# Attention scores from the third pair on in three passes of rounded parts, with the parts made on POOL

## The chip, the cores and the metric

The kernel runs on one core of a Trainium2 chip. The metric is the device time of one execution, in microseconds (us). The time before the change is the median of three runs, 790.76 us (790.69 to 790.87).

## What is computed

A causal attention block is followed by two mixing blocks; all tensors are float32. Sizes: batch 2, 12 heads, sequence 448, head width 64, model width 768, hidden width 3072, rank 32.

```
scores = (q @ k.T) / sqrt(64); causal mask; softmax over keys
x      = softmax(scores) @ v, heads side by side       # 2 x 448 x 768
h      = x.T @ U @ V                                    # mixes tokens
u      = x + h.T
y      = u + relu(u @ w_ch1) @ w_ch2
out    = y + relu(layernorm(y) * g @ w_ch1b) @ w_ch2b
```

## The kernel before

TensorE (PE in the profile) does nearly all of the work. The attention takes the first 99 us, the two feed-forward layers the rest.

**The attention** works on pairs of heads: 2 batches by 6 pairs are 12 pairs, numbered n = 0 to 11. A tile `qk` holds q and k of a pair, transposed: partitions 0 to 63 are the first head, 64 to 127 the second. `a_load(n)` (L307) fetches it with two DMAs on SP's queue; the pool has three buffers. `a_scores(n)` (L328) multiplies four blocks of 112 query rows with the keys up to the diagonal, for both heads: eight matmuls with 448, 336, 112 and 224 columns in turn, each 64 rows deep, so that the two heads use the two halves of the array's rows. Their operands are plain float32. A float32 matmul shows in the trace as two MATMUL records, so one pair has 16. At its end `a_scores(n)` starts `a_load(n + 3)`.

`a_max` (L349) on DVE (VectorE) then adds the mask and takes row maxima, eight instructions per pair at L357. `a_exp` (L366) on ACT (ScalarE) takes the exponentials. `a_transpose` (L379) turns the weights over on PE (20 transposes, L392), copies them out on DVE (L396) and ACT (L401), and has POOL (GpSimd) add a small number to the row sums (`rd`, L382). `a_values` (L403) multiplies with v (L412). `a_tokens` (L419), `a_mix1` (L447) and `a_mix2` (L466) lay the result out by tokens and begin the mixing with U and V; `a_mix1` has ACT and DVE write a small tile `ts` (L459, L462), which the last matmul of `a_mix2` (L476) reads.

**The order of the work** is written by hand. The loop over n (L533) handles pair n's transposes and values, the tokens of pair n - 1, the mixing of pair n - 2 and the scores and maxima of pair n + 2 in the same round. The prologue computes the scores of pairs 0 and 1. One round from n = 3 on takes the same 8.12 us each time.

**Weights ahead of time.** The feed-forward weights arrive as 64-bit numbers in tiles `raw`, fetched on SP's queue by `load` (L79). ACT takes their magnitude (L126), and DVE narrows them to float32 in four steps over 768 columns (`narrow`, L130): two tensor_scalar instructions on one tensor (L138, L141), then two scalar_tensor_tensor instructions on two tensors (L143, L145). In the attention's rounds `weights(9999, 2, ...)` (L406) puts at most two such steps at the end of a round of DVE.

**The other matmuls** (L490, L681, L815) already work with high and low parts: a tensor is rounded to the type F32R (high part), the rest is stored as a second F32R tensor (low part), and three passes high x high, high x low and low x high are summed. An F32R matmul shows as one MATMUL record. `low_part` (L199) makes the low part, in the attention on POOL, later on DVE.

The scores before, as they are issued:

```python
    for (h, i), (acc, o) in sorted(at.items(), key=lambda t: turns.index(t[0][1])):
        w = (i + 1) * Q
        r = slice(h * D, (h + 1) * D)
        nc.tensor.matmul(
            acc[:Q, o:o + w], t[r, 0, i * Q:(i + 1) * Q], t[r, 1, :w], start=True, stop=True,
        )
    a_load(n + 3)
```

Of the kernel before, what the change touches and what calls it, by code (L numbers as in the profile page):

```python
# [9 lines left out]
F32R = mybir.dt.float32r  # L10
# [3 lines left out]
ALU = mybir.AluOpType  # L14
PSUM = bass.MemoryType.PSUM

B, H, S, D = 2, 12, 448, 64
# [4 lines left out]
P = 128  # L22
Q = 112
# [20 lines left out]
def block_kernel(ctx: ExitStack, tc: tile.TileContext, qk, v, U, V4, w1a, w2a, w1b, w2b, g_ln, out):  # L44
    nc = tc.nc
    f32 = lambda ap: ap.bitcast(F32)
# [13 lines left out]
    attn = ExitStack()  # L60
    attn_c = attn.enter_context(tc.tile_pool(name="attn_c", bufs=1))

    def bank(name):
        return ps.tile([P, 512], F32, tag="bank", name=name)
# [44 lines left out]
    def magnitude():  # L109

        if len(started) > (not now[0]) or not (to_start and raws):
            return False
        m, n = to_start[0]
        if m and n % 2 == 0:
            if len(x_open) >= X_BUFS and x_open[-X_BUFS]:
                return False
            x_s[0] = x_w.tile([P, 2, DM], F32, tag="x", name=f"x{m}_{n}")
            x_open.append(2)
        to_start.pop(0)
        t, rows, cols = raws.pop(0)  # L120
        low, high = (t[:rows, :cols].bitcast(U32).rearrange("p (n t) -> p n t", t=2)[:, :, i] for i in range(2))
        x = x_s[0][:, n % 2] if m else uv[n][:rows, :cols]
        if m:
            x_of[m, n] = len(x_open) - 1
        act(cols)
        nc.scalar.activation(x, high.bitcast(F32), AF.Abs)  # L126
        started.append((x, x_s[0], low, high))
        return True
# [21 lines left out]
    def whole(steps):  # L150
        while True:
            try:
                next(steps)
            except StopIteration as e:
                return e.value
# [138 lines left out]
                return  # L294

    qk_p = attn.enter_context(tc.tile_pool(name="qk_p", bufs=2))
    s_p = attn.enter_context(tc.tile_pool(name="s_p", bufs=6))
    pt_p = attn.enter_context(tc.tile_pool(name="pt_p", bufs=6))
    x_p = attn.enter_context(tc.tile_pool(name="x_p", bufs=2))
    ot_p = attn.enter_context(tc.tile_pool(name="ot_p", bufs=2))  # L300
    sel_p = attn.enter_context(tc.tile_pool(name="sel_p", bufs=1))

    sc_t, qk_t, v_t, s_t, den_t, pt_t, x_t, o_t, rd_t, nm_t = ({} for _ in range(10))
    pairs = [(b, p) for b in range(B) for p in range(NP)]
    NPT = len(pairs)

    def a_load(n):  # L307

        if n >= NPT:
            return  # L310
        r = qk_t[n] = qk_p.tile([P, 2, S], F32, tag="qk", name=f"qk{n}", bufs=3)
        src = qk[n].rearrange("p (a h s) -> p a h s", a=2, h=2)
        for part in (slice(0, 2 * Q), slice(2 * Q, S)) if n == 0 else (slice(0, S),):
            for h in range(2):
                rows = slice(h * D, (h + 1) * D)
                (nc.scalar if h and n == 0 else nc.sync).dma_start(out=r[rows, :, part], in_=src[rows, :, h, part])
# [8 lines left out]

    JOBS = [[(h, 3, 0)] for h in range(2)] + [[(h, 2, 0), (h, 0, 336)] for h in range(2)] + [[(h, 1, 0)] for h in range(2)]

    def a_scores(n):  # L328
        if n >= NPT:
            return  # L330
        t = qk_t.pop(n)
        sc_t[n] = [bank("sc") for _ in JOBS]
        at = {(h, i): (acc, o) for acc, job in zip(sc_t[n], JOBS) for h, i, o in job}
        turns = (3, 2, 0, 1) if n else (1, 0, 2, 3)
        for (h, i), (acc, o) in sorted(at.items(), key=lambda t: turns.index(t[0][1])):
            w = (i + 1) * Q
            r = slice(h * D, (h + 1) * D)
            nc.tensor.matmul(  # L338
                acc[:Q, o:o + w], t[r, 0, i * Q:(i + 1) * Q], t[r, 1, :w], start=True, stop=True,
            )  # L340
        a_load(n + 3)


    TURNS = [(m, h, i, o) for m, job in enumerate(JOBS) for h, i, o in job]
# [1 line left out]
    def turns_of(n):  # L346
        return TURNS if n else sorted(TURNS, key=lambda t: (t[1], (1, 0, 2, 3).index(t[2])))

    def a_max(n, between=None):  # L349

        if n < NPT:
            nm = nm_t[n] = small.tile([Q, 2, NQ], F32, tag="nm", name=f"nm{n}")
            sb = s_t[n] = [s_p.tile([Q, OFF[NQ]], F32, tag="s", name=f"s{n}_{h}") for h in range(2)]
            accs = sc_t.pop(n)
            for k, (m, h, i, o) in enumerate(turns_of(n)):
                w = (i + 1) * Q
                nc.vector.tensor_tensor_reduce(  # L357
                    sb[h][:, OFF[i]:OFF[i + 1]], accs[m][:Q, o:o + w], mask[:, S - w:], -0.125, 3.0e38,
                    ALU.add, ALU.min, accum_out=nm[:, h, i:i + 1],
                )  # L360
                if k == 5 and between:
                    next(between)
        if between:
            whole(between)

    def a_exp(n):  # L366

        if n >= NPT:
            return
        den = den_t[n] = small.tile([Q, 2, NQ], F32, tag="den", name=f"den{n}")  # L370
        nm, sb = nm_t.pop(n), s_t[n]
        for _, h, i, _ in turns_of(n):
            s = sb[h][:, OFF[i]:OFF[i + 1]]
            nc.scalar.activation(  # L374
                s, s, AF.Exp, bias=nm[:, h, i:i + 1], scale=-1.0, accum_out=den[:, h, i:i + 1]
            )
            yield
# [69 lines left out]
    def a_mix1(n):  # L447

        b, p = pairs[n]
        x = x_t[b, p // 2]  # L450
        c = (p % 2) * P
        acc = bank("t4")
        for i in range(NQ):
            nc.tensor.matmul(acc[:, :P], u_r[:, i * P:(i + 1) * P], x[:, i, c:c + P], start=i == 0, stop=i == NQ - 1)  # L454
        acc_t = acc
        t = ts[b][:, p * P:(p + 1) * P]

        def parts():
            nc.scalar.copy(t, acc_t[:, :P])  # L459
            yield  # L460
            r = slice(2 * R, P)
            nc.vector.tensor_tensor(t[r], acc_t[r, :P], f32(t[r]), ALU.subtract)  # L462

        return parts()
# [35 lines left out]
    with tc.manual_schedule():  # L500
# [15 lines left out]
        t = wraw.tile([P, DM], I64, tag="raw64", name="raw64")  # L516
# [11 lines left out]
        for _ in a_exp(0):  # L528
            pass
        a_scores(1)  # L530
        a_max(1)
        early, low = {}, None
        for n in range(NPT):  # L533
            exps = a_exp(n + 1)
            if n == 0:
                magnitude()
                magnitude()
            a_transpose(n, exps, low)
            if n:
                a_tokens(n - 1)  # L540
            mix = a_mix1(n - 2) if n > 1 else None
            a_scores(n + 2)
            if n == 0:
                u_n = whole(narrow())[0].rearrange("p (i r) -> p i r", i=NQ)
                nc.gpsimd.tensor_copy(
                    u_r.rearrange("p (i g r) -> p i g r", i=NQ, g=4), u_n.unsqueeze(2).to_broadcast([Q, NQ, 4, R])
                )
                v_n = whole(narrow())[0]
            if n == NPT - 1:
                early[0] = bank("h")  # L550
                mm1(early[0], 0, 0, S, range(KC // 2))
            if n >= NPT - 2:
                next(mix)
            for _ in range(3):
                next(exps, None)
            high_parts(nc.gpsimd)
            a_max(n + 2, mix)
            for _ in exps:
                pass
            if n == NPT - 1:  # L560
                mm1(early[0], 0, 0, S, range(KC // 2, KC))
            a_values(n)
            if n == 0:

                v_r = bank("vr")
                for g in range(4):
                    nc.tensor.matmul(  # L567
                        v_r[:, g * Q:(g + 1) * Q], sel[:, g].rearrange("p a r -> p (a r)"), v_n,
                        start=g == 0, stop=g == 3, skip_group_check=True,
                    )  # L570
                nc.scalar.copy(vs, v_r[:, :S])
                for g in (1, 3):
                    r = slice(g * R, (g + 1) * R)
                    nc.vector.tensor_tensor(vs[r], v_r[r, :S], f32(vs[r]), ALU.subtract)
                nc.gpsimd.memset(f32(vz).bitcast(U32), 0)
                nc.gpsimd.tensor_copy(vz[:, 0, :64], f32(vs[:, 384:448]))
                nc.gpsimd.tensor_copy(vz[:, 1, 64:], f32(vs[:, 0:64]))
            a_load_v(n + 3)
            if n > 1:
                low = a_mix2(n - 2)  # L580
# [284 lines left out]
        for layer in range(2):  # L865
            building, s_t = None, []
            for g in range(NG):
# [35 lines left out]
                if (layer, g) in FAST:  # L903
# [7 lines left out]
                    turns = [(0, 1), (0, 2), (0, 6), (0, 5), (0, 7), (1, 1), (0, 4), (1, 2), (0, 3), (1, 6), (1, 5), (1, 7)]  # L911
# [14 lines left out]
                else:  # L926
# [7 lines left out]
                    for slot, (j, half) in enumerate(jobs):  # L934
                        n = ns[j]
# [3 lines left out]
                        if half == 0 and n in early:  # L939
                            acc = early[n]  # L940
                        else:
                            acc = bank("h")
# [109 lines left out]
```

## Time and profile before

| | |
|---|---|
| median of three runs | 790.76 us |
| the profiled execution's own time | 789.65 us |
| its span, first to last instruction | 787.9 us |
| PE busy | 782.8 us, 99% of the span |
| DVE busy | 638.1 us, 81% |
| ACT busy | 406.6 us, 52% |
| POOL busy | 109.7 us, 14% |
| granted TensorE clock, mean over the span | 1.000 |

The profiled execution took 1.11 us less than the median, and 1.75 us of its time lie outside the span. Busy time of an engine counts instructions that overlap once. A PE record's start is when it was let go, and its end is modelled, so an array that waits a short while can still read as busy.

### The profile page before, as it was taken

Reading aid. Unit: us, or ns where it says so; the run is one execution under the profiler, and the core shown is the slowest. Engines: PE = TensorE matmul, PEld = TensorE weight load, DVE = VectorE, ACT = ScalarE, POOL = GpSimd, SP = SyncE. Lnnn points to the kernel's source line nnn. Section 1 sums busy time; section 2 is a strip of 40 time slices with the busy share of each in tenths; the row PEclk is TensorE's granted clock in tenths of the full one; section 3 lists DMA queues with packets and bytes.
Section 4 is the critical chain, followed back from the end, with each engine's and each line's share of the span. In section 5 each row is a group of like instructions: output and inputs, shape, how many; then the busy total and the mean of one; then the engine's idle time right before and its main releaser. Section 6 shows DMA issues by size and latency. Waiting matters only on the chain.

```text
span 787.9 us, 12054 instructions
## 1 busy us (share of the span) xinstructions
PE 782.8 (99%) x4510; PEld 728.7 (92%) x4510; DVE 638.1 (81%) x1114; ACT 406.6 (52%) x817; POOL 109.7 (14%) x136
## 2 busy tenths in 40 slices
PE   9999999999999999999999999999999999999998
PEld 7777789998999999999999999989999999999997
DVE  6888869979988969789698789988989698697532
ACT  6988936353555464364463544635554544643510
POOL 1010130110210300301202501201202202103000
PEclk9999999999999999999999999999999999999999
DMA  8564344892683862944927425946946828628234
GB/s 203 171 166 120 94 144 162 182 239 80 152 230 105 222 172 83 272 110 124 289 78 268 164 81 153 236 118 179 225 132 165 216 92 221 172 96 182 39 124 157
DMA packets 39258, 126.45 MB, mean 160 GB/s; under 512 B 4752, under 2 KB 14816, under 8 KB 39200
## 3 DMA queue, kind: packets, MB, share of 16 engines
q1 hardware_dynamic: 25936, 97.24, 37.0%
q0 software_dynamic: 12656, 27.99, 21.1%
q8 instruction: 35, 0.57, 0.3%
q10 hardware_dynamic: 608, 0.46, 0.2%
q14 instruction: 23, 0.19, 0.1%
HBM read 89.88 MB, written 35.78 MB: 159 GB/s over the span
## 4 chain that ended last, share of the span: by engine, by line
PE 99%; DVE 0%; ACT 0%; issue 0%; POOL 0%; POOLq 0%
PE y L681 44%; PE pA L815 15%; PE h L490 15%; PE pB L815 7%; PE pC L815 4%; PE sc L338 3%; PE pv L412 3%; PE tr L392 3%; PE t L454 1%; PE uT L472 1%; PE xt L424 1%; PE zT L747 1%; PE warm L525 0%; PE uT L476 0%; PE y L710 0%; PE vr L567 0%
## 5 line engine op out<-in xcount | busy, mean ns | idle before, releaser
L681 PE MATMUL y<-w,h 128*128 128x384 f32 x2016 | 354.9, 334 | 0.0
L681 PEld LDWEIGHTS y<-w,h 128*128 128x128 f32 x2016 | 349.7, 188 | 1.3 <-DVE u L758 0.3
L490 PE MATMUL h<-u,w 128*128 128x384 f32 (+2 forms) x576 | 118.3, 364 | 0.0
L201 DVE TENSOR_TENSOR w<-x,w 128x768 fp32r<-128x768 f32 x93 | 87.1, 951 | 35.2 <-ACT w L190 35.2
L490 PEld LDWEIGHTS h<-u,w 128*128 128x128 f32 x576 | 104.9, 188 | 10.7
L126 ACT ACTIVATE x<-raw 128x768 f32<-128x768 f32 x96 | 86.7, 911 | 48.9 <-DMA raw<-in_w2b 25.0
L698 POOL DMA_DIRECT2D ysum<-part x54 | 47.2, 875 | 419.2 <-ACT part L697 417.4
L143 DVE SCALAR_TENSOR_TENSOR x<-raw,x 128x768 uint32<-128x768 uint32 x96 | 91.9, 957 | 2.6
L145 DVE SCALAR_TENSOR_TENSOR x<-raw,x 128x768 uint32<-128x768 uint32 x96 | 91.7, 955 | 2.1
L697 ACT COPY part<-y 128x384 f32<-128x384 f32 x108 | 46.5, 484 | 86.6 <-PE y L681 55.3
L190 ACT CAST w<-x 128x768 fp32r<-128x768 f32 x96 | 76.4, 838 | 9.6 <-PE h L490 4.5
L138 DVE TENSOR_SCALAR x<-x 128x768 f32<-128x768 f32 x96 | 54.7, 569 | 12.8 <-ACT x L126 12.6
L141 DVE TENSOR_SCALAR x<-x 128x768 uint32<-128x768 uint32 x96 | 53.6, 558 | 1.9
L374 ACT ACTIVATE s<-s,nm 112x336 f32<-112x336 f32 (+2 forms) x96 | 50.7, 536 | 0.0
L357 DVE CUSTOM_DVE_ANT_0 s<-sc,mask 112x336 f32<-112x336 f32 (+2 forms) x96 | 36.5, 445 | 12.8 <-PE sc L338 12.8
L823 ACT COPY u<-pA 128x448 f32<-128x448 f32 x32 | 17.1, 534 | 49.1 <-PE pA L815 45.9
L692 POOL DMA_DIRECT2D ysum<-part x32 | 29.7, 1071 | 58.5 <-ACT part L691 58.5
L765 ACT ACTIVATE h<-h 128x384 fp32r<-128x384 f32 (+2 forms) x32 | 17.5, 546 | 37.9 <-PE h L490 37.9
L767 DVE SCALAR_TENSOR_TENSOR h<-u,h 128x448 fp32r<-128x448 f32 x32 | 20.0, 626 | 17.7 <-ACT h L765 17.7
L815 PE MATMUL pC<-u,w 128*128 128x448 f32 x144 | 32.1, 367 | 0.0
L815 PE MATMUL pB<-u,w 128*128 128x448 f32 x144 | 32.0, 366 | 0.0
L815 PE MATMUL pA<-u,wt 128*128 128x448 f32 x144 | 32.0, 366 | 0.0
(105 smaller groups left out, 970.3 us busy)
## 6 DMA issues: line engine op xcount, KB each, us to landing
ysum<-part POOLq DMA_DIRECT2D x54, 384.0 KB, 7.0
raw<-in_w1a SPq DMA_DIRECT2D x24, 768.0 KB, 6.5
raw<-in_w2a SPq DMA_DIRECT2D x24, 768.0 KB, 4.9
raw<-in_w1b SPq DMA_DIRECT2D x24, 768.0 KB, 5.8
raw<-in_w2b SPq DMA_DIRECT2D x24, 768.0 KB, 4.8
ysum<-part POOLq DMA_DIRECT2D x32, 192.0 KB, 6.6
y<-ysum SPq DMA_DIRECT2D x14, 384.0 KB, 4.0
qk<-in_qk SPq DMA_DIRECT2D x22, 224.0 KB, 3.9
```

What stands on the lines that cost most here:

```text
L126: nc.scalar.activation(x, high.bitcast(F32), AF.Abs)
L138: nc.vector.tensor_scalar(x, x, LEAST, GREATEST, ALU.max, ALU.min)
L141: nc.vector.tensor_scalar(bits, bits, 5, 2, ALU.logical_shift_left, ALU.logical_shift_right)
L143: nc.vector.scalar_tensor_tensor(bits, low, 29, bits, ALU.logical_shift_right, ALU.bitwise_or)
L145: nc.vector.scalar_tensor_tensor(bits, high, 0xC0000000, bits, ALU.bitwise_and, ALU.bitwise_or)
L190: nc.scalar.copy(w[:, 0], x)
L201: engine.tensor_tensor(w[:, 1], x, f32(w[:, 0]), ALU.subtract)
L374: nc.scalar.activation(s, s, AF.Exp, bias=nm[:, h, i:i + 1], scale=-1.0, accum_out=den[:, h, i:i + 1])
L490: nc.tensor.matmul(acc[:, :width], w[:, a, k, c0:c0 + P], u[:, c, kk, t0:t0 + width], start=kk == a == c == 0, stop=kk == KC - 1 and a == 1,)
L681: nc.tensor.matmul(accs[k][:, :c1 - c0], hs[j][:, a, tb * P:(tb + 1) * P], w2_s[ns[j]][:, c, c0:c1], start=first and j == a == c == 0, sto ...
L698: nc.gpsimd.dma_start(out=y_sum[tb], in_=part, accum_op=ALU.add)
L815: nc.tensor.matmul(acc[:, :S], w[:, a, slot, kk * P:(kk + 1) * P], operand(c, kk), start=first and kk == a == c == 0, stop=kk == 2 and a = ...
```

## The change

From the third pair on (n of 2 and more), q and k are no longer multiplied as float32. A new function `a_split(n)` has POOL round the whole tile to F32R (one copy of 128 x 896) and subtract that from the original (one tensor_tensor of 128 x 896); the result is a tile `qs` with four F32R parts, in a pool of two buffers. `a_scores` then issues three passes for each block: high x high, high x low, low x high, the two heads in turn within a pass. That is 24 F32R matmuls in the place of 8 float32 ones. Pairs 0 and 1 keep the float32 matmuls.

`a_load(n + 3)` moves from the end of `a_scores(n)` to the end of `a_split(n)` for these pairs, since the split is now the last reader of `qk`. The split of pair 2 comes at the end of the prologue, that of pair n + 3 right behind the scores of pair n + 2. In the changed kernel's program the attention's later lines stand 19 to 21 lines further down: the rd instruction is L401, the scores are L357, the loads are L317.

```diff
     qk_p = attn.enter_context(tc.tile_pool(name="qk_p", bufs=2))
+    qs_p = attn.enter_context(tc.tile_pool(name="qs_p", bufs=2))
...
+    def a_split(n):
+
+        if not 2 <= n < NPT:
+            return
+        r = qk_t.pop(n)
+        t = qs_t[n] = qs_p.tile([P, 2, 2, S], F32R, tag="qs", name=f"qs{n}")
+        nc.gpsimd.tensor_copy(t[:, 0], r)
+        nc.gpsimd.tensor_tensor(t[:, 1], r, f32(t[:, 0]), ALU.subtract)
+        a_load(n + 3)
+
     def a_scores(n):
         if n >= NPT:
             return
-        t = qk_t.pop(n)
         sc_t[n] = [bank("sc") for _ in JOBS]
         at = {(h, i): (acc, o) for acc, job in zip(sc_t[n], JOBS) for h, i, o in job}
-        turns = (3, 2, 0, 1) if n else (1, 0, 2, 3)
-        for (h, i), (acc, o) in sorted(at.items(), key=lambda t: turns.index(t[0][1])):
+        if n < 2:
+            t = qk_t.pop(n)
+            passes = [(t[:, 0], t[:, 1])]
+            a_load(n + 3)
+        else:
+            t = qs_t.pop(n)
+            passes = [(t[:, a, 0], t[:, c, 1]) for a, c in ((0, 0), (0, 1), (1, 0))]
+        for i in (3, 2, 0, 1) if n else (1, 0, 2, 3):
             w = (i + 1) * Q
-            r = slice(h * D, (h + 1) * D)
-            nc.tensor.matmul(
-                acc[:Q, o:o + w], t[r, 0, i * Q:(i + 1) * Q], t[r, 1, :w], start=True, stop=True,
-            )
-        a_load(n + 3)
+            for m, (q, k) in enumerate(passes):
+                for h in range(2):
+                    acc, o = at[h, i]
+                    r = slice(h * D, (h + 1) * D)
+                    nc.tensor.matmul(
+                        acc[:Q, o:o + w], q[r, i * Q:(i + 1) * Q], k[r, :w],
+                        start=m == 0, stop=m == len(passes) - 1,
+                    )
...
         a_max(1)
+        a_split(2)
...
             a_scores(n + 2)
+            a_split(n + 3)
```

**SP's queue, at the loads of pairs 3 to 5** (`qk_183`, `qk_220`, `qk_291` before; `qk_178`, `qk_215`, `qk_240` and, for pair 6, `qk_319` now; two DMAs each; in brackets the semaphores waited for). Before:

```order
L316 DMA qk_183<-in_qk 64x2x448 [waits DMAHW1_49,DMAHW2_49,DMAHW0_49,PE_49]
L316 DMA qk_183<-in_qk 64x2x448 [waits DMAHW1_49]
L316 DMA qk_220<-in_qk 64x2x448 [waits DMAHW2_49,PE_49]
L316 DMA qk_220<-in_qk 64x2x448 [waits DMAHW3_49]
L316 DMA qk_291<-in_qk 64x2x448 [waits DMAHW4_49,PE_49]
L316 DMA qk_291<-in_qk 64x2x448 [waits DMAHW5_49]
L82 DMA raw_298<-in_w1a 128x768 [waits DMAHW6_49]
```

Now:

```order
L317 DMA qk_178<-in_qk 64x2x448 [waits DMAHW3_49,DMAHW4_49,DMAHW0_49,Pool_49]
L317 DMA qk_178<-in_qk 64x2x448 [waits DMAHW1_49]
L317 DMA qk_215<-in_qk 64x2x448 [waits DMAHW2_49,PE_49]
L317 DMA qk_215<-in_qk 64x2x448
L317 DMA qk_240<-in_qk 64x2x448 [waits PE_49]
L317 DMA qk_240<-in_qk 64x2x448 [waits DMAHW5_49]
L317 DMA qk_319<-in_qk 64x2x448 [waits DMAHW1_49,DMAHW6_49,DMAHW0_49,Pool_49]
L317 DMA qk_319<-in_qk 64x2x448 [waits DMAHW7_49]
L82 DMA raw_326<-in_w1a 128x768
```

The load of pair 3 waits for POOL (the split of pair 2) where it waited for PE (the scores of pair 0), and the load of pair 6 now stands ahead of the first weights.

**POOL, from the prologue to the third round** (`rd` is L382's tile before and L401's now; `qs` the new tiles of pairs 2 to 5). Before:

```order
L510 COPY sel<-ident 128x512
L382 TENSOR_SCALAR rd_236<-den_197 112x8 [waits Activation_49]
L545 COPY u_r<-uv_103 112x512 [waits DVE_49]
L575 MEMSET vz 128x256
L576 CAST vz<-vs 128x64 [waits DVE_49,Activation_49,Pool_49]
L577 CAST vz<-vs 128x64
L382 TENSOR_SCALAR rd_348<-den_244 112x8
L382 TENSOR_SCALAR rd_443<-den_356 112x8 [waits Activation_49]
```

Now:

```order
L335 CAST qs_237<-qk_154 128x896 [waits DMAHW4_49,DMAHW3_49]
L336 TENSOR_TENSOR qs_237<-qk_154,qs_237 128x896 [waits Pool_49]
L401 TENSOR_SCALAR rd_245<-den_200 112x8 [waits Activation_49]
L335 CAST qs_316<-qk_178 128x896 [waits DMAHW1_49,DMAHW0_49]
L336 TENSOR_TENSOR qs_316<-qk_178,qs_316 128x896 [waits Pool_49]
L566 COPY u_r<-uv_103 112x512 [waits DVE_49]
L596 MEMSET vz 128x256
L597 CAST vz<-vs 128x64 [waits DVE_49,Activation_49,Pool_49]
L598 CAST vz<-vs 128x64
L401 TENSOR_SCALAR rd_376<-den_253 112x8
L335 CAST qs_454<-qk_215 128x896 [waits DMAHW3_49,DMAHW2_49,PE_49]
L336 TENSOR_TENSOR qs_454<-qk_215,qs_454 128x896 [waits Pool_49]
```

From the first round on, each `rd` is followed by the two instructions of a split: rd of pair n by the split of pair n + 3.

## Rows read from the trace of the kernel before

**Rows 1.** The page, busy time of each engine, its share and instructions.

```profile
PE 782.8 (99%) x4510; PEld 728.7 (92%) x4510; DVE 638.1 (81%) x1114; ACT 406.6 (52%) x817; POOL 109.7 (14%) x136
```

**Rows 2.** Chain of waits in order of time: start us, us, what.

```profile
12.87 2.10 PE sc L338 x16
...
20.44 2.66 PE sc L338 x15
...
41.51 1.92 PE tr L392 x20
...
44.77 2.08 PE sc L338 x16
```

**Rows 3.** Windows, three rounds: us, then PE, PEld, DVE, ACT, POOL, clock, DMA.

```profile
33.23:41.35 8.12, 8.12 (x70) 6.08 (x69) 6.86 (x25) 6.61 (x22) 0.23 (x1) 1.00 0.46 108
41.35:49.47 8.12, 8.12 (x70) 6.08 (x69) 7.53 (x25) 6.61 (x22) 0.23 (x1) 1.00 0.68 213
...
65.71:73.83 8.12, 8.12 (x70) 6.08 (x69) 7.53 (x25) 6.61 (x22) 0.23 (x1) 1.00 0.64 183
```

**Rows 4.** Timeline of DVE, 44.6 to 49.2 us: start, us, instruction, idle before.

```profile
45.73 0.62 DVE L357 CUSTOM_DVE_ANT_0 s<-sc,mask 112x448 f32<-112x448 f32 x1 [0.33 <-PE sc L338]
...
48.81 0.29 DVE L462 TENSOR_TENSOR ts<-t,ts 64x128 fp32r<-64x128 f32 x1
```

**Rows 5.** Timeline of PE at 700 us, F32R matmuls.

```profile
699.72 1.19 PE L815 MATMUL pA<-u,wt 128*128 128x448 f32 x5
700.76 2.02 PE L815 MATMUL pB<-u,w 128*128 128x448 f32 x9
```

**Rows 6.** Groups by form: xcount, busy us, mean ns, idle before.

```profile
L681 PE MATMUL y<-w,h 128*128 128x256 f32 x12 | 1.6, 282 | 0.0
...
L201 POOL TENSOR_TENSOR w<-x,w 128x768 fp32r<-128x768 f32 x3 | 5.5, 1834 | 21.4 <-ACT w L190 21.4
...
L510 POOL COPY sel<-ident 128x512 f32<-128x512 f32 x1 | 0.6, 611 | 0.0
```

**Rows 7.** SP's timeline, then the landings of all qk loads, then ACT's timeline.

```profile
6.20 1.18 SPq L316 DMA_DIRECT2D qk<-in_qk  x2
...
16.24 1.89 SPq L82 DMA_DIRECT2D raw<-in_w1a  x2
...
DMA to landing us min/median/max: 2.7/3.9/5.7
...
31.14 0.94 ACT L126 ACTIVATE x<-raw 128x768 f32<-128x768 f32 x1
```

**Rows 8.** Timeline of POOL in the rounds.

```profile
31.34 0.23 POOL L382 TENSOR_SCALAR rd<-den 112x8 f32<-112x8 f32 x1 [6.99 <-ACT s L374]
39.59 0.23 POOL L382 TENSOR_SCALAR rd<-den 112x8 f32<-112x8 f32 x1 [8.02 <-ACT s L374]
...
56.27 1.83 POOL L201 TENSOR_TENSOR w<-x,w 128x768 fp32r<-128x768 f32 x1 [8.33 <-ACT w L190]
...
64.57 0.23 POOL L382 TENSOR_SCALAR rd<-den 112x8 f32<-112x8 f32 x1 [5.97 <-ACT s L374]
```

**Rows 9.** Timeline of DVE, weight steps in the rounds.

```profile
32.90 0.56 DVE L138 TENSOR_SCALAR x<-x 128x768 f32<-128x768 f32 x1
...
41.02 0.96 DVE L143 SCALAR_TENSOR_TENSOR x<-raw,x 128x768 uint32<-128x768 uint32 x1
...
57.26 1.26 DVE L138 TENSOR_SCALAR x<-x 128x768 f32<-128x768 f32 x1
...
65.38 0.96 DVE L143 SCALAR_TENSOR_TENSOR x<-raw,x 128x768 uint32<-128x768 uint32 x1
```

**Rows 10.** Line L138 over the span (duration ns min/median/max); DVE and POOL at 435 us.

```profile
L138 DVE TENSOR_SCALAR x<-x x96: 546/553/1260, 32.9 to 723.6; 128x768 f32<-128x768 f32 x96
...
435.14 1.02 DVE L967 TENSOR_TENSOR y<-y,y 128x384 f32<-128x384 f32 x2
...
435.51 1.84 POOL L738 TENSOR_TENSOR z<-z,g_b 128x768 f32<-128x768 f32 x1 [1.34 <-ACT z L737]
```

More of the change, by code (lines that the diff above doesn't have):

```diff
@@ L301, in block_kernel @@
     sel_p = attn.enter_context(tc.tile_pool(name="sel_p", bufs=1))
-    sc_t, qk_t, v_t, s_t, den_t, pt_t, x_t, o_t, rd_t, nm_t = ({} for _ in range(10))
+    sc_t, qk_t, qs_t, v_t, s_t, den_t, pt_t, x_t, o_t, rd_t, nm_t = ({} for _ in range(11))
     pairs = [(b, p) for b in range(B) for p in range(NP)]
```

## The prediction

> **What bounds the kernel now.** I read the page first. PE is busy for 782.8 of 787.9 us [rows 1], so what lengthens or shortens PE's work shows in the end, wherever it lies, unless PE waits for something else in its place. The change touches the attention alone, so I read that next, in the chain of waits and in windows of one round each. The chain stays on PE throughout, and the scores are 2.08 us of each round [rows 2]. The windows show how near the others are. A round takes 8.12 us; DVE works 6.86 us of the round from 33.23 on and 7.53 us of those from 41.35 and 65.71 on, which leaves it 1.26 and 0.59 us [rows 3]. So DVE has little to give.
>
> A second loop is nearly as long as PE's own. The scores start at 44.77 [rows 2], DVE's first maximum starts at 45.73, having waited 0.33 us for them, and the last DVE step of the round, `ts`, ends at 48.81 + 0.29 = 49.10 [rows 4]. The matmul that reads `ts` is issued right there, ahead of the next transposes. A shorter score group helps only as far as its first block also comes earlier.
>
> **The change, part by part.**
>
> *The passes.* Before, a group takes 2.08 us: four cycles for each of 448 + 336 + 224 + 112 = 1120 columns at 2.4 GHz (granted clock 1.00, rows 3) are 1.87 us, with both heads side by side; 0.21 us are edges. Now there are three F32R passes. Full-height F32R matmuls give the spacing: 448 columns (700.76 - 699.72) / 5 = 0.208 us [rows 5]; 256 columns (1.6 - 0.282) / 11 = 0.120 us [rows 6]. On that line 336 columns take 0.157 and 224 take 0.105 us. For 112 columns the line gives 0.054, but each pass loads 112 columns of weights; 20 transposes that do the same took 1.92 us [rows 2], 0.096 each, which I take. Three passes: 3 x (0.208 + 0.157 + 0.105 + 0.096) = 1.70, with the edges 1.91 us: 0.17 us less for each of ten pairs. The DVE loop gains less: its first block takes 3 x 0.208 = 0.62 us where four cycles took 0.75, so 0.12 us. I take 0.15 us a round. The ends: 0 and 0.19. No row shows F32R passes below 256 columns, or on half of the rows; rivals 3 and 4 price that.
>
> *The split.* Neither size is in the trace. POOL's copy of 512 columns took 611 ns, its subtraction of 768 columns 1834 ns [rows 6]; by columns that is 1.07 and 2.14 us for 896, together 3.21 us a pair. In the steady rounds the split of pair n + 3 starts behind `rd` of pair n, more than a round ahead of its scores, so it is not waited for. At the start it is.
>
> *The first splits.* The load of pair 2 is issued in two halves from 6.20 on, the second about 6.8; with the median of 3.9 us to landing [rows 7] it is there at 10.7. Copy to 11.8, subtraction to 13.9. PE reaches the scores of pair 2 at 12.87 [rows 2]; the first pass needs only high parts, the second the low part of k, at about 13.2. So PE waits some 0.75 us. The load of pair 3 now stands behind that split on SP: it reuses its buffer, and waits for POOL. Its second half goes out at 13.9 + 0.7 = 14.6, lands at 18.5 (17.3 to 20.3 with the shortest and the longest landing), and the split ends at 21.7 (20.5 to 23.5). PE comes to these scores at 20.44 + 0.75 - 0.15 and wants the low part at 21.3: 0.4 us of waiting, between 0 and 2.2. The group at 20.44 already took 2.66 instead of 2.08 us, which may swallow part. From pair 4 on the loads lead. The start costs 1.15 us, between 0.5 and 3.0.
>
> *Queues that are passed.* SP's first weights go out behind the load of pair 6, which waits for the second split: from 16.24 to about 23. They take up to 1.9 us to issue and a few to land; ACT reads the first at 31.14 [rows 7], so this is covered by one to two microseconds. If that cover went, each microsecond would delay L138 by one.
>
> *POOL beside DVE.* This is the largest term. L138 takes 0.55 us; the one at 57.26 took 1.26, beginning while POOL's subtraction of 56.27 to 58.10 ran and ending 0.42 us behind its end [rows 8 to 10]. A DVE pass was held until POOL had finished. Two passes with one operand in PSUM, at 435.14, went through in 1.02 us under a POOL multiplication [rows 10]. L143, with two operands in SBUF, never meets POOL here. L138 handles a column in 0.72 ns, L143 in 1.25: both draw two SBUF elements in about that time, the PSUM readers one. So I place L143 and L145 with L138: held. The other end is not held at all. As a rule of its own: "A DVE instruction with two SBUF inputs contends with a GpSimd instruction that reads SBUF" (the Trainium skill, SBUF — State Buffer, section Who interferes with whom). By it the sum is the one below; if only L138's kind is held it is rival 1's; no run here shows L143 beside POOL.
>
> Now the places. `rd` ends at 31.57, 39.82 and 64.80 [rows 8]; the splits behind it last until 34.8, 43.0 and 68.0. L138 starts at 32.90, L143 at 41.02 and 65.38 [rows 9], inside all three.
> - 32.90: held 1.9 us; the round behind it has 1.26 us to spare: 0.65 us.
> - 41.02: the subtraction began at 40.9; held 2.0 us, 0.59 us to spare: 1.4 us.
> - 65.38: held 0.5 us by the copy; then L143 and the subtraction change places, and L145 either slips in or waits 2.1 us more. 0 or 2.0 us; I take 1.0.
>
> Together 3.05 us, between 0 and 4.05.
>
> **The sum.** Start +1.15, held DVE +3.05, and 0.15 us gained in the seven rounds without a collision, -1.05: +3.15 us. Against the profiled execution's 789.65 that is 792.8; this execution lies 1.11 us under the median of 790.76, so I forecast the median: **793.9 us**. What a measurement here can tell from no change is about 0.2%, 1.6 us: 789.2 to 792.3.
>
> **Rivals.**
> 1. *Not slower: two-operand passes are not held.* Then only 32.90 costs: 1.15 + 0.65 - 9 x 0.15 = +0.45, 791.2 us. It decides at the split of pair 7: if L143 still takes 0.96 us while POOL subtracts, this holds. For it: no row shows such a pass held. Against: the drawing rates above.
> 2. *Faster: POOL is quick and nothing is held.* If the splits of pairs 2 and 3 end before 13.2 and 21.3 the start is free, and ten groups gain up to 0.19: -1.9, 788.9 us. Against: the copy and subtraction would have to be a quarter quicker than the rows, and L138 at 57.26 was held.
> 3. *The short passes are not one cycle a column.* The shortest F32R pass in the trace has 256 columns. If 224 and 112 take the four cycles of float32, 0.373 and 0.187 us, the group is 3 x (0.208 + 0.157 + 0.373 + 0.187) + 0.21 = 2.99 us: 0.91 us more, ten times, and the start: +10.2, 801.0 us. PE is then so late that DVE's holding is covered. The change would not do what it says.
> 4. *The heads no longer run side by side.* All F32R matmuls in the trace use the full height. In turn, a group is 6 x 0.566 + 0.21 = 3.61 us: +1.53, ten times, and the start's wait mostly covered: +16, 806.8 us. Against: the float32 groups run side by side, on the same rows.
>
> **How the numbers follow.** Forecast 0.52, rival 1 0.20, rival 2 0.08, rival 3 0.13, rival 4 0.07. The forecast's own range is 791.8 to 797.2: the start from 0.5 to 3.0, the third collision at 0 or 2.0, POOL a tenth quicker or slower. The range for 8 in 10 takes in rivals 1 and 3 and leaves out 2 and 4: 789.4 to 801.2. Slower by over 0.2%: forecast 0.47, rivals 3 and 4 0.20, a little of 1, together 0.68. Within: 0.05 of the forecast, 0.17 of rival 1, 0.02 else: 0.24. Faster: 0.08.
>
> **What would show it.** Scores from pair 2 on: 24 records, first starts 0.21 us apart in pairs; groups near 1.9 us in the steady rounds (3.0: rival 3; 3.6: rival 4). PE idle ahead of, or inside, the groups at about 13 and 21 us, released by POOL. POOL's two lines at about 1.1 and 2.1 us. L138 and L143 or L145 of 2 us and more in three rounds, followed by a PE wait for a DVE copy or `ts`; rounds without a collision near 7.97 us. From 100 us on, all as before, only shifted. The forecast is wrong if the splits end ahead of their first readers, if L143 keeps 0.96 us, or if the steady rounds are longer than 8.12 us.

## The result

The changed kernel takes **794.54 us** (median of 6 runs, 793.36 to 795.59) against 790.54 us for the kernel before (6 runs, 789.73 to 790.87) on the same chip: 1.0053 times the time, 95% interval 1.0043 to 1.0063. It is 4.0 us slower; 793.9 was forecast. The profiled execution of the changed kernel took 794.69 us, its span is 792.9 us at a granted clock of 1.000.

The page's busy times are to be compared with [rows 1]. PE and POOL have more to do, but PE's 0.9 us more of work is far from the 5.0 us by which this span is longer:

```profile
PE 783.7 (99%) x4590; PEld 734.0 (93%) x4590; DVE 643.2 (81%) x1114; ACT 406.9 (51%) x817; POOL 140.8 (18%) x156
```

The windows of four rounds of the changed kernel are to be compared with [rows 3]; the columns are the same (time, then PE, PEld, DVE, ACT, POOL, clock, DMA):

```profile
34.86:43.60 8.74, 8.58 (x79) 6.86 (x78) 8.61 (x25) 6.61 (x22) 3.90 (x4) 1.00 0.83 206
43.60:52.51 8.91, 8.75 (x79) 6.84 (x78) 8.64 (x25) 6.61 (x22) 3.43 (x4) 1.00 0.43 138
52.51:60.48 7.97, 7.97 (x79) 6.59 (x78) 5.97 (x22) 7.78 (x24) 2.04 (x2) 1.00 0.64 155
68.45:78.51 10.06, 8.88 (x79) 6.84 (x78) 9.79 (x25) 6.60 (x22) 6.20 (x5) 1.00 0.32 111
```

A round that meets nothing now takes 7.97 us where it took 8.12. Three rounds take 8.74, 8.91 and 10.06 us; in them DVE is busy all but 0.13 to 0.27 us, with the same 25 instructions that needed 6.86 or 7.53 us before. Some DVE instruction there takes longer. DVE's timeline, and below it POOL's, name them (start, length):

```profile
34.52 2.42 DVE L138 TENSOR_SCALAR x<-x 128x768 f32<-128x768 f32 x1
...
43.26 2.18 DVE L143 SCALAR_TENSOR_TENSOR x<-raw,x 128x768 uint32<-128x768 uint32 x1
...
68.11 1.55 DVE L143 SCALAR_TENSOR_TENSOR x<-raw,x 128x768 uint32<-128x768 uint32 x1
69.69 2.73 DVE L145 SCALAR_TENSOR_TENSOR x<-raw,x 128x768 uint32<-128x768 uint32 x1
```

```profile
34.41 2.10 POOL L336 TENSOR_TENSOR qs<-qk,qs 128x896 fp32r<-128x896 f32 x1
...
42.53 2.09 POOL L336 TENSOR_TENSOR qs<-qk,qs 128x896 fp32r<-128x896 f32 x1
...
67.92 0.93 POOL L335 CAST qs<-qk 128x896 fp32r<-128x896 f32 x1
68.93 2.68 POOL L336 TENSOR_TENSOR qs<-qk,qs 128x896 fp32r<-128x896 f32 x1
```

L138 took 0.56 us there before, L143 0.96 [rows 9]. Each long pass ends 0.4 to 0.8 us after POOL's instruction: L138 at 36.94, POOL at 36.51; L143 at 45.44, POOL at 44.62; L145 at 72.42, POOL at 71.61. DVE holds POOL too: the subtraction at 68.93 began inside L143 and took 2.68 us instead of 2.10, and the copy at 61.71, in a round that lost nothing, began inside L141 (61.59 to 62.15) and took 1.23 us instead of 0.93.

The chain of waits of before ran on PE alone in the rounds [rows 2]. Now, followed back from the end, it leaves PE at 78.14 and runs over DVE to 72.54, where the page loses it: from the copies out of PSUM through x and the maxima to `ts`, which PE's next matmul reads (start, length, what):

```profile
74.26 0.60 DVE x L449
...
77.84 0.30 DVE ts L481
78.14 0.04 issue
78.19 0.47 PE uT L495
...
81.91 1.86 PE sc L357 x24
```

The start is read from PE's timeline, with the idle time and its releaser in brackets, and POOL's:

```profile
12.99 0.46 PE L357 MATMUL sc<-qs 64*112 64x448 f32 x2
14.05 1.72 PE L357 MATMUL sc<-qs 64*112 64x448 f32 x22 [0.60 <-POOL qs L336]
...
21.18 0.45 PE L357 MATMUL sc<-qs 64*112 64x448 f32 x2
23.11 1.74 PE L357 MATMUL sc<-qs 64*112 64x448 f32 x22 [1.48 <-POOL qs L336]
```

```profile
10.87 0.94 POOL L335 CAST qs<-qk 128x896 fp32r<-128x896 f32 x1 [8.21 <-DMA qk<-in_qk]
11.89 2.10 POOL L336 TENSOR_TENSOR qs<-qk,qs 128x896 fp32r<-128x896 f32 x1
...
19.95 0.93 POOL L335 CAST qs<-qk 128x896 fp32r<-128x896 f32 x1 [5.62 <-DMA qk<-in_qk]
20.97 2.08 POOL L336 TENSOR_TENSOR qs<-qk,qs 128x896 fp32r<-128x896 f32 x1
```

The first pass of pairs 2 and 3 runs, the second waits for the low part of k.

**The account.** Taken from the first transpose of each round to that of the next, the two profiled executions differ so (us):

| round | 0 | 1 | 2 | 3 | 4 | 5, 6 | 7 | 8, 9 | 10 |
|---|---|---|---|---|---|---|---|---|---|
| before | 7.37 | 7.14 | 8.17 | 8.12 | 8.12 | 8.12 each | 8.12 | 8.12 each | 6.04 |
| after | 8.34 | 8.09 | 8.04 | 8.74 | 8.91 | 7.97 each | 10.06 | 7.96, 7.98 | 6.04 |
| difference | +0.97 | +0.95 | -0.13 | +0.62 | +0.79 | -0.30 | +1.94 | -0.30 | 0 |

Round 0 also begins 0.16 us earlier (10.39 instead of 10.55), so PE is 4.3 to 4.4 us later at the end of the attention. The other 0.7 us of the span's 5.0 come later; the last section tells where.

### The profile page after: what moved, and what is told of

It is laid out like the page before. It is cut to its first block, busy times and chain, and to the rows that moved or that the text cites. A ratio compares the mean times of both kernels' runs of the same rounds, so it can differ in the third digit from the quotient of the medians.

```text
span 792.9 us, 12226 instructions
## 1 busy us (share of the span) xinstructions
PE 783.7 (99%) x4590; PEld 734.0 (93%) x4590; DVE 643.2 (81%) x1114; ACT 406.9 (51%) x817; POOL 140.8 (18%) x156
## 4 chain that ended last, share of the span: by engine, by line
PE 89%; DVE 1%; ACT 0%; issue 0%
PE y L702 44%; PE pA L836 15%; PE h L509 14%; PE pB L836 7%; PE pC L836 4%; PE pv L431 1%; PE tr L411 1%; PE zT L768 1%; PE t L473 1%; PE sc L357 0%; DVE s L376 0%; PE y L731 0%; PE uT L491 0%; PE uT L495 0%; PE xt L443 0%; DVE u L500 0%
## 5 line engine op out<-in xcount | busy, mean ns | idle before, releaser
L143 DVE SCALAR_TENSOR_TENSOR x<-raw,x 128x768 uint32<-128x768 uint32 x96 | 93.7, 976 | 2.6
L145 DVE SCALAR_TENSOR_TENSOR x<-raw,x 128x768 uint32<-128x768 uint32 x96 | 93.5, 974 | 2.1
L138 DVE TENSOR_SCALAR x<-x 128x768 f32<-128x768 f32 x96 | 56.9, 592 | 12.0 <-ACT x L126 11.7
L141 DVE TENSOR_SCALAR x<-x 128x768 uint32<-128x768 uint32 x96 | 53.7, 560 | 1.9
L836 PE MATMUL pA<-u,w 128*128 128x448 f32 x144 | 32.2, 368 | 0.0
```

Of the source, the lines that this page charges most:

```text
L138: nc.vector.tensor_scalar(x, x, LEAST, GREATEST, ALU.max, ALU.min)
L141: nc.vector.tensor_scalar(bits, bits, 5, 2, ALU.logical_shift_left, ALU.logical_shift_right)
L143: nc.vector.scalar_tensor_tensor(bits, low, 29, bits, ALU.logical_shift_right, ALU.bitwise_or)
L145: nc.vector.scalar_tensor_tensor(bits, high, 0xC0000000, bits, ALU.bitwise_and, ALU.bitwise_or)
L836: nc.tensor.matmul(acc[:, :S], w[:, a, slot, kk * P:(kk + 1) * P], operand(c, kk), start=first and kk == a == c == 0, stop=kk == 2 and a = ...
```

## The experiments

Each is compared with runs of the kernel before on the same chip.

| kernel | median, us | before, us | ratio, 95% interval |
|---|---|---|---|
| the change | 794.54 | 790.54 | 1.0053 (1.0043 to 1.0063) |
| the change again | 794.57 | 790.51 | 1.0051 (1.0038 to 1.0065) |
| split made but not read | 794.27 | 789.81 | 1.0055 (1.0041 to 1.0068) |
| memsets in its place | 790.17 | 789.81 | 1.0005 (0.9996 to 1.0013) |
| passes alone | 788.54 | 789.81 | 0.9985 (0.9976 to 0.9994) |
| change from pair 4 on | 792.12 | 789.81 | 1.0033 (1.0021 to 1.0045) |
| late split | 790.75 | 790.51 | 1.0005 (0.9996 to 1.0014) |
| late split from pair 4 on | 788.83 | 790.51 | 0.9978 (0.9970 to 0.9987) |
| loads behind the scores | 794.54 | 790.51 | 1.0053 (1.0040 to 1.0065) |
| a fourth buffer | 794.76 | 789.87 | 1.0068 (1.0054 to 1.0081) |

**1. The split, made but not read.**

```diff
 def a_split(n):
-        r = qk_t.pop(n)
+        r = qk_t[n]
...
-        a_load(n + 3)
...
 def a_scores(n):
...
+        t = qk_t.pop(n)
+        passes = [(t[:, 0], t[:, 1])]
...
+        a_load(n + 3)
```

> POOL makes the split of pairs 2 to 11 at the same places as in the change, but nobody reads it: the scores stay float32 on q and k, and the loads stand where they stood before. Theory (POOL's split holds DVE's two-operand weight passes): the three collisions remain and the passes' gain is gone, so the profile shows L138 near 2.4 us once, L143 near 2.2 and a third held pass at about 66 us; the rounds behind them are 0.6, 0.8 and 1 to 2 us longer, PE has no wait for POOL at the start, and the time is 2.4 to 3.4 us above the kernel before (793.0 to 794.0). Rival (POOL is harmless, what the change costs is the three passes and the wait at the start): within 0.3 us of the kernel before, 790.5.

The kernel is 4.46 us above before, as much as the change within the intervals. The three collisions are there, on DVE's timeline:

```profile
36.27 2.28 DVE L138 TENSOR_SCALAR x<-x 128x768 f32<-128x768 f32 x1
...
44.88 2.33 DVE L143 SCALAR_TENSOR_TENSOR x<-raw,x 128x768 uint32<-128x768 uint32 x1
...
70.18 1.23 DVE L143 SCALAR_TENSOR_TENSOR x<-raw,x 128x768 uint32<-128x768 uint32 x1
71.45 2.73 DVE L145 SCALAR_TENSOR_TENSOR x<-raw,x 128x768 uint32<-128x768 uint32 x1
```

Their rounds take 8.60, 9.06 and 9.74 us against 8.12: 3.04 us, inside the 2.4 to 3.4 expected. The rest was not expected: a fourth collision in the start. With the loads where they stood, the second split runs from 14.97 to 18.12, and there DVE narrows the small matrices U and V. One pass (L141 on 112 columns, some 0.2 us by itself) took 1.98, and PE waited for the last of them. PE's waits between 8 and 100 us are this one (longer than 0.1 us; total, times, longest):

```profile
PE vr L582 <- DVE uv L145: 2.1, 1, 2.1
```

The start of this profile must be read with care. Behind that wait TensorE's granted clock was 0.50, the lower of its two levels (1.2 GHz), from 21.0 to 24.1 us, and the transposes there took 3.46 us instead of 2.08:

```profile
20.21 3.46 PE L405 MATMUL tr<-ident,s 112*112 112x112 f32 x20
```

So rounds 0 and 1 lose 3.4 us in this execution, about 1.7 of it in the two groups at the lower clock (the transposes and L437, 0.93 instead of 0.60). It took 796.08 us, the longest of the six, and is the only one whose mean granted clock is below 1.00. The median's 4.46 us less the 3.04 of the three rounds leaves 1.4 for the start.

**2. Memsets in place of the split.** Does POOL hold DVE because it is busy, or because it reads?

```diff
-        nc.gpsimd.tensor_copy(t[:, 0], r)
-        nc.gpsimd.tensor_tensor(t[:, 1], r, f32(t[:, 0]), ALU.subtract)
+        nc.gpsimd.memset(f32(t[:, 0]).bitcast(U32), 0)
+        nc.gpsimd.memset(f32(t).bitcast(U32), 0)
```

> As the run with the unread split, but POOL writes the same tiles with two memsets (896 and 1792 columns) instead of the copy and the subtraction: it is busy for about as long (estimate from the memset of 448 columns in 0.47 us: 0.95 + 1.9 = 2.8 us) and reads nothing from SBUF. The scores are float32, so the computation is that of before. Theory (what holds DVE is that POOL reads SBUF while DVE reads two elements): L138 keeps 0.55 us and L143 0.96, the time is that of before, 790.5. Rival (any POOL instruction that uses SBUF holds the two-operand passes): L138 and L143 of 1.5 us and more at 33, 41 and 65 us, the time 2 to 3 us above before.

Theory and rival were each half right. DVE's timeline, then POOL's:

```profile
33.73 1.65 DVE L138 TENSOR_SCALAR x<-x 128x768 f32<-128x768 f32 x1
...
41.86 0.96 DVE L143 SCALAR_TENSOR_TENSOR x<-raw,x 128x768 uint32<-128x768 uint32 x1
...
66.21 0.96 DVE L143 SCALAR_TENSOR_TENSOR x<-raw,x 128x768 uint32<-128x768 uint32 x1
```

```profile
33.37 1.60 POOL L336 MEMSET qs<- 128x1792 uint32 x1
...
41.63 1.60 POOL L336 MEMSET qs<- 128x1792 uint32 x1
...
66.61 1.60 POOL L336 MEMSET qs<- 128x1792 uint32 x1
```

L138, which reads one tensor, is held by a POOL instruction that only writes: it ends at 35.38, the memset at 34.97. L143, which reads two, is not: 0.96 us with the memset of 41.63 to 43.23 over all of it. So the two kinds of DVE pass are held under different conditions. The Trainium skill (SBUF — State Buffer, section Who interferes with whom) separates them the same way: a one-source DVE instruction in a mode that uses both port pairs contends with GpSimd altogether, one with two SBUF inputs only with a GpSimd instruction that reads SBUF. No run here shows in which mode L138 works. L138's 1.1 us here cost no round: the window of its round reads 8.12, since DVE had 1.26 us to spare there [rows 3].

**3. The passes alone.**

```diff
 def a_split(n):
-        if not 2 <= n < NPT:
-            return
...
-        if n < 2:
+        if n < 4:
...
-            t = qs_t.pop(n)
+            t = qs_t[2]
...
-            a_split(n + 3)
```

> Pairs 2 and 3 keep float32; pairs 4 to 11 take three F32R passes, all on one tile that POOL made once, of pair 2, in the prologue (so the scores of those pairs are of the wrong pair); POOL has no other split to make. Theory (the passes gain 0.15 us in each round and POOL's work is the whole loss): rounds from pair 4's scores on take 7.97 us, eight times 0.15 us, so 1.2 us below before: 789.3. Rival (the passes themselves cost, by the wait of the first pass or of DVE): rounds of 8.12 or more and no gain: 790.5 or above.

1.27 us below before (0.5 to 1.9 by the interval), 1.2 expected. The windows of the rounds in which the change has its first two collisions:

```profile
33.58:41.56 7.98, 7.98 (x79) 6.58 (x78) 6.86 (x25) 6.61 (x22) 0.23 (x1) 1.00 0.86 234
41.56:49.54 7.98, 7.98 (x79) 6.58 (x78) 7.52 (x25) 6.61 (x22) 0.23 (x1) 1.00 0.33 100
```

The passes gain what was forecast, and PE is busy throughout.

**4. The change from pair 4 on.**

```diff
-        if not 2 <= n < NPT:
+        if not 4 <= n < NPT:
...
-        if n < 2:
+        if n < 4:
...
-            a_load(n + 3)
...
+        if n < 4:
+            a_load(n + 3)
```

> The change, but pairs 2 and 3 keep float32 scores, so that the split begins with pair 4. Theory: the wait at the start (measured 0.97 + 0.95 us in the first two rounds of the change) goes and two gains of 0.15 us go with it; the held passes stay (0.6 + 0.8 + 1.9 us) against six gains of 0.15: 2.0 to 2.5 us above before, 792.5 to 793.0, about 1.7 us below the change. Rival (the start's delay only moves, as the same work comes later anyway): the same time as the change, 794.5. A third way: without the delay POOL meets DVE at other places, and the third collision costs 0 or 2.

2.3 us above before (1.7 to 3.6), in the expected place: rounds 3, 4 and 7 take 8.74, 8.91 and 10.04 us, and those between and behind them 7.97. The start's delay does not move elsewhere; without it the collisions cost the same. Against the run with the passes alone this kernel differs by POOL's splits and by the place of the loads that they release, and by 3.6 us (792.12 - 788.54); in the profiles the three rounds account for it (27.69 us against 23.95). That is what the splits cost from pair 4 on.

**5. The late split.**

```diff
 def a_values(n):
...
         nc.vector.reciprocal(rd, rd)
+        if n + 4 < NPT:
+            gate = small.tile([Q, 2, NQ], F32, tag="gate", name=f"gate{n}")
+            nc.gpsimd.tensor_scalar(gate, rd, 1e-9, None, ALU.add)
+            a_split(n + 4)
...
-            a_split(n + 3)
+            if n == 0:
+                a_split(3)
```

> The change, but from pair 4 on POOL waits, through a small instruction that reads the reciprocals of pair n - 4, until DVE's weight steps of that round are through, and splits only then, a round earlier than its reader needs. The splits of pairs 2 and 3 stay where they are. Theory (the steady loss is nothing but the meeting of POOL's split and the weight steps): L138 0.55 us (1.3 beside L201 as before), L143 and L145 0.96 throughout, all rounds from the third on at 7.97 us, so the start's +1.9 and eight gains of 0.15 remain: 0.7 us above before, 3.3 below the change. Rival (POOL holds whatever DVE pass it meets, so a later split only moves the loss to the maxima and copies): the rounds stay at 8.0 to 9 us and the time near the change's.

0.24 us above before (0.3 below to 1.1 above), 0.7 expected. No pass is held (L143 at 44.55 and 68.51 takes 0.96, L138 at 36.58 takes 0.56), and rounds 3 to 9 take 7.97 to 8.00 us. The maxima and copies of DVE now run beside the splits and lose nothing. In the start one new wait came: `rd` of pair 1 stands behind the split of pair 4 on POOL, and DVE's reciprocal waited 1.32 us for it.

The start of the profiled execution is no fair measure here either. Rounds 0 and 1 take 18.09 us in it, 3.6 more than before, where 1.9 was expected. Behind PE's wait of 1.72 us for the low part of k of pair 3 the granted clock was 0.50 from 25.0 to 28.0 us, and the two groups of matmuls there took 1.6 us longer than in the change (1.74 and 2.11):

```profile
23.57 2.03 PE L357 MATMUL sc<-qs 64*112 64x448 f32 x22 [1.72 <-POOL qs L336]
25.53 3.42 PE L435 MATMUL pv<-pt,v 112*64 112x448 f32 x16
```

This execution took 792.46 us. It and two others of the eleven (791.89 and 793.05) show a mean granted clock below 1.00; the eight at 1.00 lie between 789.37 and 790.85.

**6. The late split from pair 4 on.** Experiment 5 with `4 <= n`, `n < 4` and the moved load of experiment 4, and no split of pairs 2 and 3.

> The late split, and pairs 2 and 3 keep float32 scores. Theory: neither the start's wait nor a held pass is left; eight gains of 0.15 us: 1.2 us below before (ratio 0.9985), as with the passes alone. Rival (the split in another place meets something else, the maxima, the copies or x): at or above before.

1.7 us below before (1.0 to 2.4): faster than both kernels. The windows of the three rounds that collided in the change, POOL's work among them:

```profile
32.36:40.35 7.99, 7.99 (x79) 6.62 (x77) 6.86 (x25) 6.60 (x22) 3.52 (x4) 1.00 0.55 146
40.35:48.34 7.99, 7.99 (x79) 6.62 (x77) 7.52 (x25) 6.61 (x22) 3.58 (x5) 1.00 0.53 161
64.30:72.30 8.00, 8.00 (x79) 6.60 (x78) 7.52 (x25) 6.60 (x22) 3.58 (x5) 1.00 0.40 138
```

POOL is busy 3.5 to 3.6 us of each and DVE's sums are those of before. In the profiled execution half a microsecond of the gain lies in rounds 0 and 1, where PE does what it does in the kernel before; those rounds vary from profile to profile, so the gain of the passes themselves is nearer to 1.1 us, eight rounds by 0.14.

**7. Loads behind the scores,** to start the load of pair 3 earlier.

```diff
         if n < 2:
...
-            a_load(n + 3)
...
+        if n < 2:
+            a_load(n + 3)
```

> The change, with the loads of pairs 3 and 4 started behind the matmuls of scores 0 and 1 as in the kernel before; the load of pair 3 then waits for the scores of pair 0 and goes out at about 8.8 instead of 14.0 us. Theory (a late load is the greater part of the start's cost, but POOL's second split then runs at 15 to 18 us and holds DVE's narrowing of U and V there): PE's wait of 1.7 us inside the scores of pair 3 goes, DVE's narrowing passes of 0.2 to 0.3 us become 1 to 2 us, PE waits for them ahead of the matmuls of vr, and the time stays within 1 us of the change. Rival (the load is all): the first two rounds are 1.7 us shorter and the time is 1.7 us below the change, 0.3% above before.

This edit did not do what it was meant to: SP still sends the load of pair 3 at 13.55, when POOL's first split ends (11.43 + 2.10), as if pair 3 still got the buffer of pair 2. It decides nothing on the start.

**8. A fourth buffer,** so that the load of pair 3 need not wait.

```diff
-tag="qk", name=f"qk{n}", bufs=3)
+tag="qk", name=f"qk{n}", bufs=4)
...
-name="s_p", bufs=6
+name="s_p", bufs=5
```

> The change with four buffers for q and k instead of three (and five instead of six for the weights of softmax, to make room), so that the load of pair 3 waits for no split and goes out at about 8.8 us instead of 14. Theory (the late load makes PE's wait of 1.5 us inside the scores of pair 3; an early one brings POOL's second split to 14 to 18 us, where DVE narrows U and V, as in the run with the unread split): PE's wait for POOL at pair 3 is gone, DVE's narrowing passes of 0.2 to 0.3 us take 1 to 2 us, PE waits 1 to 2 us for them ahead of vr, and the time is within 1 us of the change, 794.5. Rival (the load is all of it): nothing takes the wait's place, and the time is 1.5 us below the change, 793.0, 0.3% above before.

The load of pair 3 goes out at 9.23 us. The time stays, 4.9 us above before. PE's wait inside the scores of pair 3 is gone and another stands ahead of `vr`; PE's waits between 8 and 34 us, then DVE's timeline, then POOL's:

```profile
PE vr L588 <- DVE uv L145: 0.9, 1, 0.9
PE sc L357 <- POOL qs L336: 0.9, 1, 0.9
```

```profile
15.67 0.88 DVE L143 SCALAR_TENSOR_TENSOR uv<-raw,uv 128x112 uint32<-128x112 uint32 x1
16.59 2.14 DVE L145 SCALAR_TENSOR_TENSOR uv<-raw,uv 128x112 uint32<-128x112 uint32 x1
```

```profile
15.46 0.96 POOL L335 CAST qs<-qk 128x896 fp32r<-128x896 f32 x1 [0.97 <-DMA qk<-in_qk]
16.51 2.08 POOL L336 TENSOR_TENSOR qs<-qk,qs 128x896 fp32r<-128x896 f32 x1
```

A DVE pass of 0.28 us took 2.14 beside the subtraction. Rounds 0 and 1 take 9.60 and 7.26 us, together 2.35 us more than before; the change's took 1.92 more. The late load had kept POOL away from DVE's narrowing. The buffer taken from the weights of softmax was not tried by itself, but the rounds from the third on take the times of the change within 0.04 us.

**9. The change again.**

> The change itself, once more, with more runs. It should stand at 1.005 of before, 4 us above. Two things are read from its profile: whether the held passes lie at the same three places (L138 near 2.4 us, L143 near 2.2, L143 1.5 and L145 2.7; theory: they do, since the order is fixed) and whether six of the eight stretches of 36 mixing matmuls at 448 columns take 0.207 us each instead of 0.2025 again (if it belongs to the program, yes, 0.7 us; if to the one execution, no).

The passes are held at the same places: L138 2.42 us, L143 2.17, L143 1.53, L145 2.73. Rounds 0 and 1 cost 1.25 us more than before here (7.92 and 7.84) against 1.92 in the first profile: POOL got the load of pair 3 at 19.61 instead of 19.95 us, and PE left round 1 at 26.46 instead of 26.82. The start varies with the landing of its loads. Of the mixing stretches more below.

## Why the forecast held, step by step

The forecast named the mechanisms and their sign; the start was sized 0.6 to 0.9 us too small, the held passes 0.3 us, and one cost was not in it.

- **The passes: right.** A group was to take 1.91 us and takes 1.86; a free round was to take 7.97 and does. That leaves no room for four cycles a column in the short passes (2.99 us) or for heads in turn (3.61): rivals 3 and 4 fall. The group is 0.22 us shorter than before and the round 0.15; the forecast had set the round below the group, since DVE's loop shortens only by its first block. The free round bears that out: DVE's first maximum starts 0.90 us behind the scores (55.84 and 56.74) where it started 1.04 behind them (52.82 and 53.86), and `ts` ends at 60.10, right ahead of the matmul at 60.16 that reads it.
- **POOL: right within a tenth for the split.** Copy and subtraction were put at 1.07 and 2.14 us and took 0.93 and 2.10: the subtraction scaled by columns, the copy was cheaper than its row suggested. Rival 2 falls: the splits end after their readers want them.
- **The start: right in kind, too small.** Pair 2's wait was to be 0.75 us; the second pass follows the first by 14.05 - 12.99 = 1.06 instead of 0.2, so 0.85. Pair 3's was to be 0.4 between 0 and 2.2; 23.11 - 21.18 less 0.2 is 1.7. The step that failed is the landing of that load, taken with the median latency at 18.5: POOL waited for it until 19.95, inside the 17.3 to 20.3 given. So the term, put at 1.15 with the gains of these rounds counted apart, was 0.97 + 0.95 - 0.16 + 2 x 0.15 = 2.06 in this execution and, by the same sum, 1.70 in the other profile of the change. The two waits together are 2.6 us: the group that took 2.66 us before [rows 2] swallowed some 0.6 of them, as the forecast allowed.
- **Held DVE passes: the mechanism right, the sum near by offsets.** Forecast 0.65, 1.4 and 1.0, measured 0.62, 0.79 and 1.94: 3.35 instead of 3.05. The second was too high because L143 began 0.73 us into the subtraction, not 0.1: the forecast had kept the times of before, but `rd` came 1.62 us later than before and L143 2.24. DVE had moved against POOL by 0.6 us, about as much as the held L138 had cost the round ahead. The third was a middle value between 0 and 2.0; L143 was held by the copy, the subtraction by L143, and L145 waited for all of it, the long end, in both profiles of the change and in experiments 1, 4, 7 and 8 alike. Where both engines' orders are fixed, such a meeting is no even chance.
- **Why they are held: half right.** I placed L143 with L138 because both draw two SBUF elements in about the same time. Beside a POOL that reads, both are held, so the term stands and rival 1 falls. But the memsets show that they are not one kind: L138 is held by a writing POOL as well, L143 is not.
- **Queues passed: right.** SP sends the first weights after the load of pair 6, around 24 us, and no round waits for a weight.
- **"From 100 us on, all as before, only shifted": not quite.** Between 100 us and the end the changed kernel's profiled execution loses a further 0.7 us, its repetition 1.0 us.
- **The sum.** Forecast +3.15 us; by PE's place at the end of the attention the change cost 4.3 us in its first profile and 4.0 in the second, with 0.7 to 1.0 us behind it. The medians, 4.0 us apart, are less than these sums because the profiled execution of before lies 0.9 us under its median and that of the change 0.15 over its own.

That the splits are the loss is shown: without them the passes gain 1.27 us, with them late the loss is gone, and unread they bring the same three collisions back.

## What to carry to other kernels

An idle engine is not a free one: before work goes to POOL, list which DVE instructions will run beside it, sort them into one-source passes over SBUF, two-source passes over SBUF and readers of PSUM, and place POOL's work beside the last kind; a tiny POOL instruction that reads what DVE writes behind its weight steps was enough to do so. A held instruction shows as a long one, not as a wait: compare an instruction's longest time with its median. And when one delay is removed, ask what it had kept apart.

## What was not expected of the hardware

- DVE's one-source pass L138 is held by a POOL memset (0.55 to 1.65 us), its two-source pass L143 is not (0.96), while POOL's copy or subtraction holds both (L138 2.42, L143 2.18). DVE instructions that read PSUM kept their times beside the splits (in experiment 6, beside the subtraction of 43.48 to 45.61, 0.68 us for x and 0.62 for the maxima, as before).
- In two of the profiles, those of experiments 1 and 5, the granted TensorE clock fell to 0.50 in the start for some 3 us, behind a wait of PE of 2.06 and 1.72 us, and cost some 1.7 and 1.6 us more. In the change's own profile the start is at 1.00; one of its six executions, at 795.59 us, has a mean of 0.998. In these executions a wait of PE cost nearly twice its length; in most others of the same kernels the mean granted clock is 1.00.
- The mixing matmuls behind the attention have two speeds. In the changed kernel, from PE's timeline:

```profile
238.99 2.02 PE L836 MATMUL pA<-u,w 128*128 128x448 f32 x9
240.85 2.02 PE L836 MATMUL pA<-u,wt 128*128 128x448 f32 x9
```

and in the kernel before:

```profile
234.69 1.99 PE L815 MATMUL pA<-u,w 128*128 128x448 f32 x9
236.51 1.99 PE L815 MATMUL pA<-u,wt 128*128 128x448 f32 x9
```

Nine of them take 1.86 us in the one and 1.82 in the other, 0.207 and 0.2022 us each, at a granted clock of 1.00. Of the eight stretches of 36 such matmuls, none is at the slower speed in the profile of before, six in the first profile of the change, all eight in the second and in experiment 7, four or five in the late splits, none in the others, the fourth buffer among them. That is some 0.13 us a stretch by PE's place ahead of and behind it, and accounts for the 0.7 to 1.0 us behind the attention. The sixteen shorter stretches of 18 go at the slower speed in every profile but those of the two late splits, where all go at the faster. It does not follow POOL's work, since the unread split shows none of it, and the same program had six and eight slow stretches. What sets it stays open.
